# One attention-decode kernel, one core: the large loads move from SyncE's queue to GpSimd's, with an engine's rows joined in one packet

## The chip, the cores and the metric

The kernel runs on one core of one Trainium2 chip. Its time is the device time of one execution in microseconds (us); three executions of the kernel before gave 1303.61 to 1304.71, with a median of 1303.97. A profile is one further execution, recorded by the hardware profiler. A core has a matrix engine (TensorE, in the profile PE, its weight loads PEld), VectorE (DVE), ScalarE (ACT), GpSimd (POOL), SyncE (SP), and 16 DMA engines which bring data from device memory (HBM) to the core's own memory (SBUF, 128 partitions). A load is handed over by one of SP, ACT and POOL, each of which has a queue of its own that it works through in order; the 16 DMA engines then move the data. A load of 128 partitions gives each DMA engine eight rows.

## The reference, cut to what matters

Two tokens (B = 2) of width 512 go through a cached attention block and a two-layer MLP, in f32.

```
y  = layernorm(x);  q = (y @ wq) -> 2 x 32 heads x 128
scores = q . k_cache * 128**-0.5        # k_cache: 2 x 32 x 8192 x 128
o  = softmax(scores) . v_cache          # v_cache: the same shape
h  = x + o @ wo                         # wo: 4096 x 512
h2 = h + gelu(layernorm(layernorm(h)) @ w1 + b1) @ w2 + b2   # 512 -> 1792 -> 512
```

K and V are 268 MB each, and each element is used once. All else together is some 25 MB.

## The kernel before, in words

The work is cut into 32 units: a unit i is a pair of heads g of one token b, so units come in twos (b = 0, then b = 1). The K of a unit is a tile of 128 partitions, 64 KB in each (8 MB), and so is its V. There are three such slots of SBUF (`kv`), taken in turn: wq, K0, K1, V0, K2, V1, K3, V2 and so on, then wo, the last V and the MLP's weights. V of a unit goes into the slot that its K leaves; K of unit i+1 goes into the slot that V of unit i-2 leaves. A load into a slot can be handed over only when the last reader of what lay there is done.

On a K tile, cut into four chunks (32 of a partition's 128 scores each), DVE multiplies a chunk by q (`multiply`, line 464), for the first three chunks POOL adds the upper 64 products of each score to the lower 64 (`halve`, line 468), and DVE sums what is left (`add_up`, line 471). DVE's order within a unit is multiply 0, multiply 1, sum 0, multiply 2, sum 1, multiply 3, sum 2, sum 3. The row maximum, a maximum over partitions (through PE), and four exponentials on ACT follow for two units together; then `values` (PE, lines 241 and 193) multiplies the weights with V. For b = 0 this is done at the end of unit b = 1, and for b = 1 in the middle of the unit after. The middle pairs' PE work is one loop.

The helper `Waits` sees each instruction and puts a semaphore wait on it for whatever it needs. Loads count on 12 semaphores in turn for the hardware queues and 12 for GpSimd's; a load also waits for the load that used its semaphore before.

Which queue hands over what: SP has wq (line 307), all K and V (line 438), wo (line 444), `wlast` (line 456), the biases (line 667), W1 (line 671), W2 (line 675) and the output (line 782). ACT has x. POOL has two gathers with an index list for the rest of wo (line 448), besides its halvings and, at the end, three small fills (lines 688, 691, 710): `zeros`, which the last head's output is written into, `lane`, a small selector, and `wb`, which PE reads in matmuls whose results are not used (`keep_warm`, lines 715 to 717, the first of them inside the last `values`, line 521). The program sets 1024 bytes of a partition aside for the descriptors that GpSimd writes (line 819). It reads the MLP's weights in the order of use: W1 in two loads, W2 in four of 7, 4, 2 and 1 rows of 2 KB in a partition.

The main loop's hand-overs are at its top (lines 601 to 610): V of unit i-1 and K of unit i+1, before any of unit i's work.

Of the kernel before, what the change touches and what calls it, by code (L numbers as in the profile page):

```python
# [22 lines left out]
GH = 3  # L23
SR = 4
LW = 4
LEFT = (((0, 3), (5, 19), (20, 30), (44, 47), (55, 56), (64, 66), (68, 94), (103, 105), (108, 109), (119, 121)),
        ((0, 2), (5, 11), (12, 30), (44, 47), (56, 57), (64, 66), (68, 95), (103, 104), (108, 109), (112, 113),
         (119, 121)))
# [2 lines left out]
def kept(left):  # L31
    at, runs, n = 0, [], 0
    for a, b in (*left, (P, P)):
        if a > at:
            runs.append((at, n, a - at))
            n += a - at
        at = b
    return runs, n
# [234 lines left out]
def tile_decode_block(nc, waits, x, k, v, wq, wo, wog, wol, w1, bias, w2, out):  # L273
    B, H, SK, DH = k.shape
    D = wq.shape[0]
    F = w1.shape[1]
    DC = D // P
# [4 lines left out]
    ROW = NS2 * DH  # L282
# [3 lines left out]
    NU = len(units)  # L286
# [10 lines left out]
    def slot():  # L297
        return kv.tile([P, ROW], F32, name="kv", tag="kv")
# [3 lines left out]
    junk = const.tile([P, 3], F32, name="junk")  # L302
# [1 line left out]
    x2 = const.tile([B, D], F32, name="x2")  # L304
    nc.scalar.dma_start(x2, x)
    wqt = slot()
    nc.sync.dma_start(wqt, wq.rearrange("(p r) n -> p (r n)", r=DC))
    wqs = wqt.rearrange("p (r n) -> p r n", r=DC)

    wlast = wts.tile([P, LW, D], F32, name="wlast")  # L310
    ident = const.tile([P, P], F32, name="ident")
# [7 lines left out]
    oall = const.tile([P, 2, 2 * GP, B], F32, name="oall")  # L319
    NQ = len(LEFT)  # L320
    og = const.tile([P, NQ * SR + LW - TH, B], F32, name="og")
    slots = [kept(x) for x in LEFT]
    first_slot = [sum(n for _, n in slots[:q]) for q in range(len(LEFT))]
    HG = H - LW
    NS = (HG - 4 * GP) * DH // SR
# [4 lines left out]
    pms = {}  # L330
    for x in LEFT:
        if x not in pms:
            pms[x] = const.tile([P, P], F32, name=f"pm{len(pms)}")
            nc.gpsimd.memset(pms[x], 0.0)
            for p0, s0, n in kept(x)[0]:
                nc.gpsimd.tensor_copy(pms[x][:, p0:p0 + n], ident[:, s0:s0 + n])
    pm = [pms[x] for x in LEFT]
    FAR = 4096.0
    ioff = const.tile([P, len(LEFT)], F32, name="ioff")
    for q in range(len(LEFT)):  # L340
# [79 lines left out]
    def make_q(g):  # L420
        QP[g] = psq.tile([P, B, DH], F32, name="qps")
        for b in range(B):
            rows, cols = of_pair(g)
            q = qs[:, (g - 1) % GH, :] if g else q2[rows, cols]
            pe.matmul(QP[g][:, b], pick[:2 * B, b, :], q, start=True, stop=True)
# [4 lines left out]
    for _ in range(SPARE):  # L430
        pe.matmul(rowacc[:, :B], wz, wz, start=True, stop=True)

    def load(src, i, parts):
        g, b = units[i]
        t = slot()
        rows = src[b, 2 * g:2 * g + 2].rearrange("h (p j) d -> (h p) (j d)", j=NS2)
        for s0, n in parts:
            nc.sync.dma_start(t[:, s0 * DH:(s0 + n) * DH], rows[:, s0 * DH:(s0 + n) * DH])
        return t

    def load_wo():
        t = slot()
        n = 2 * GP * D
        nc.sync.dma_start(t[:, :2 * n], wo)
        tv = t[:, :2 * n].rearrange("p (j c) -> p j c", j=2)
        gv = t[:, 2 * n:].rearrange("p (q r n) -> p q r n", q=len(LEFT), n=D)
        for q in range(len(LEFT)):
            nc.gpsimd.indirect_dma_start(
                out=gv[:, q].rearrange("p r n -> p (r n)"), out_offset=None,
                in_=wog,  # L450
                in_offset=bass.IndirectOffsetOnAxis(ap=gidx[:, q:q + 1], axis=0),
                bounds_check=NS - 1, oob_is_err=False)
        return tv.rearrange("p j (r n) -> p j r n", n=D), gv

    def load_last():
        nc.sync.dma_start(wlast.rearrange("p r n -> p (r n)"), wol)

    def chunk(t, c):
        return t[:, c * CH * DH:(c + 1) * CH * DH].rearrange("p (j d) -> p j d", d=DH)

    def multiply(i, c, t):
        g, b = units[i]
        kc = chunk(t, c)
        nc.vector.tensor_tensor(kc, kc, QP[g][:, b, None, :].to_broadcast([P, CH, DH]), op=ALU.mult)  # L464

    def halve(c, t):
        kc = chunk(t, c)
        nc.gpsimd.tensor_tensor(kc[:, :, 0:HP], kc[:, :, 0:HP], kc[:, :, HP:DH], op=ALU.add)  # L468
# [36 lines left out]
    def inverse(g):  # L505
        r = work.tile(list(RL[g].shape), F32, name="rl" if g < GL else "rlp")
        nc.vector.reciprocal(r, RL[g])  # L507
        RL[g] = r

    def by_head(g):  # L510
        r = RL[g]
        RL[g] = work.tile([4, 2], F32, name="rl2")
        nc.vector.tensor_scalar(RL[g], hmask, r, None, op0=ALU.mult)
# [23 lines left out]
    def head_out(g):  # L537
        op, rl = OP.pop(g), RL.pop(g)
        if g < GL:
            nc.vector.tensor_tensor(orow[:, g % GH], op[:, None, :].to_broadcast([4, 2, DH]),  # L540
                                    rl[:, :, None].to_broadcast([4, 2, DH]), op=ALU.mult)
            return
        nc.vector.tensor_tensor(otz[:, :, 0:32:16], *(x.rearrange("p (b s) -> p s b", b=B) for x in (op, rl)),
                                op=ALU.mult)

    def turn(j):
        rows = orow.rearrange("m k e d -> m (k e d)")
        if j < 4:
# [5 lines left out]
            return  # L554
        TP[j] = psm.tile([P, NQ * SR + LW - TH, 2 * B], F32, name="sm")
        at, n = (HG - 4 * GP) * DH, LW - TH
        last = rows[:, at:at + n * DH].rearrange("m (p r) -> m r p", r=n)
# [25 lines left out]
    def placed():  # L583
        nc.vector.tensor_copy(og[:, :NQ * SR], TP.pop(4))

    def project_all(wot, wgt):
        so = so2[0]
        parts = [(oall[:, j, r, :], wot[:, j, r, :]) for j in range(2) for r in range(2 * GP)]
        parts += [(og[:, q * SR + r, :], wgt[:, q, r, :]) for q in range(NQ) for r in range(SR)]
        parts += [(og[:, NQ * SR + h, :], wlast[:, h, :]) for h in range(LW - TH)]  # L590
        n = len(parts)
# [6 lines left out]

    full = [(0, NS2)]
    assert NS2 == NCH * CH  # L600
    KT, VT = {0: load(k, 0, [(0, NS2 // 2), (NS2 // 2, NS2 // 2)])}, {}
    for i, (g, b) in enumerate(units):
        if i == NU - 1:
            wot, wgt = load_wo()
        if i >= 1:
            VT[i - 1] = load(v, i - 1, full)
        if i + 1 < NU:
            KT[i + 1] = load(k, i + 1, full)
        if i == NU - 2:
            load_last()  # L610
        kt = KT.pop(i)
        S[i] = work.tile([P, NS2], F32, name="s", bufs=3)
        for c in range(NCH):
            multiply(i, c, kt)
            if c < NCH - 1:
                halve(c, kt)
            if c == 0:
                if b == 0 and g >= 1:
                    inverse(g - 1)
                if b == 1 and g >= 1:  # L620
                    head_out(g - 1)
                elif b == 1:
                    nc.vector.memset(orow, 0.0)
                if i == NU - 1:
                    turn(4)
            elif c == 1:
                if b == 0 and g >= 1:
                    by_head(g - 1)
                if b == 0 and g % GH == 1:
                    turned(max(g // GH - 1, 0))  # L630
                if i == NU - 1:
                    turned(4)
                if b == 1 and g < GL:
                    make_q(g + 1)
                    if g % GH == GH - 1:
                        stage((g + 1) // GH)
            if c >= 1:
                add_up(i, c - 1, kt, HP)
            if c == 2 and b == 0 and i >= 1:
                values(i - 1, VT.pop(i - 1))  # L640
                gather(g - 1)
                head_sum(g - 1)
                if g == GL:
                    pe.end()
            if c == 2 and i == NU - 1:
                placed()
                project_all(wot, wgt)
        add_up(i, NCH - 1, kt, DH)
        if b == 0 and g % GH == 0 and g < GL:
            pe.round()  # L650
        row_max(i)
        if i == NU - 1:
            row_sum()
        if b == 1:
            all_max(g)
            exps(g)
            values(i - 1, VT.pop(i - 1))
            total(g)
            if g % GH == 0 and g < GL:
                turn(max(g // GH - 1, 0))  # L660
# [7 lines left out]
    w1t = wt[:, 0:DC * F].rearrange("p (c f) -> p c f", c=DC)  # L668
    w1v = w1.rearrange("(p c) f -> p c f", c=DC)
    for c in range(0, DC, 2):  # L670
        nc.sync.dma_start(w1t[:, c:c + 2], w1v[:, c:c + 2])
    w2t = wt[:, DC * F:2 * DC * F].rearrange("p (t d) -> p t d", t=FT)
    w2v = w2.rearrange("(p t) d -> p t d", t=FT)
    for t, n in ((0, 7), (7, 4), (11, 2), (13, 1)):
        nc.sync.dma_start(w2t[:, t:t + n, :], w2v[:, t:t + n, :])

    inverse(GL)
    nc.scalar.activation(junk[:, 0:1], lt4[:, 0:1], AF.Sqrt)
# [154 lines left out]
```

## Time and profile before

| | |
|---|---|
| median of three runs | 1303.97 us (1303.61 to 1304.71) |
| profiled execution, from the first to the last instruction | 1302.4 us |
| moved from HBM | 561.20 MB, mean 431 GB/s |
| busy: DVE, POOL, PE | 951.3, 442.5, 386.7 us |
| chain that ended last: DMA, DVE, PE | 46%, 38%, 13% |

The runs' times include what lies around the span, so the profiled execution's 1302.4 us stands 1.6 us under the median. The busy times of the engines are to be read against the span: none comes near it. The DMA row, the mean busy share of the 16 engines, is the one that does. The profile counts one record for each row that a DMA engine moves and one for each completion.

### The profile page before, as it was taken

How to read it: one execution, taken by the hardware profiler on the slowest of the kernel's cores; microseconds unless marked ns; L12 is line 12 of the kernel's file. 1: busy time of each engine (PE TensorE's matmuls, PEld its weight loads, DVE VectorE, ACT ScalarE, POOL GpSimd, SP SyncE). 2: the span in 40 equal slices, each digit the busy share in tenths (PEclk: the TensorE clock that was granted, in tenths of full speed). 3: DMA queues.
4: the chain of work that ended last, by engine and by line, in shares of the span. 5: the costliest groups of instructions: out<-in, count | busy, mean ns of one | idle time of the engine just before them, and what ended most of it. 6: DMA issues, size and time to landing. Idle time of an engine off the chain costs nothing.

```text
span 1302.4 us, 6774 instructions
## 1 busy us (share of the span) xinstructions
PE 386.7 (30%) x2900; PEld 122.8 (9%) x2900; DVE 951.3 (73%) x411; ACT 51.7 (4%) x172; POOL 442.5 (34%) x138
## 2 busy tenths in 40 slices
PE   3105033330413314033230413323032331403358
PEld 1101000000100001010000101000010100100113
DVE  1988677779777778777778877777976777877752
ACT  0010000000000000000000000000000000000011
POOL 1444422244432234432234442224442224443320
PEclk9556566575666657566665666667566665756669
DMA  9999999999999999999999999999999999999998
GB/s 403 435 449 418 445 423 443 425 435 433 429 439 431 439 431 435 427 443 423 443 427 439 431 431 439 431 437 429 439 427 441 425 439 431 431 439 429 432 426 370
DMA packets 11420, 561.20 MB, mean 431 GB/s; under 512 B 1404, under 2 KB 1412, under 8 KB 1806
## 3 DMA queue, kind: packets, MB, share of 16 engines
q1 hardware_dynamic: 11114, 559.97, 99.5%
q0 software_dynamic: 288, 1.05, 0.2%
q8 instruction: 8, 0.13, 0.0%
q14 instruction: 6, 0.05, 0.0%
q10 hardware_dynamic: 4, 0.00, 0.0%
HBM read 562.06 MB, written 0.00 MB: 432 GB/s over the span
## 4 chain that ended last, share of the span: by engine, by line
DMA 46%; DVE 38%; PE 13%; ACT 1%; issue 1%; POOL 0%; SPq 0%; another core or an unknown queue 0%
DMA kv<-in_k_dram 41%; DVE kv L464 22%; DVE s L471 14%; PE so L241 11%; DMA kv<-in_w_dram 3%; DMA kv<-in_wq_dram 2%; PE sm L241 1%; ACT pt L495 1%; PE so L193 1%; DVE gm L483 0%; DVE mx L478 0%; DVE orow L540 0%; POOL kv L468 0%; DVE qs L418 0%; ACT nb L490 0%
## 5 line engine op out<-in xcount | busy, mean ns | idle before, releaser
L464 DVE TENSOR_TENSOR kv<-kv,qps 128x4096 f32<-128x4096 f32 x128 | 564.0, 4408 | 274.7 <-DMA kv<-in_k_dram 274.6
L468 POOL TENSOR_TENSOR kv<-kv 128x2048 f32<-128x2048 f32 x96 | 433.4, 4522 | 794.8 <-DVE kv L464 452.7
L471 DVE TENSOR_REDUCE s<-kv 128x32 f32<-128x2048 f32 (+1 forms) x128 | 357.2, 2810 | 0.7 <-POOL kv L468 0.3
L241 PE MATMUL so<-kv,pt 128*16 128x512 f32 x1920 | 277.7, 742 | 267.1 <-DMA kv<-in_v_dram 244.9
L241 PE MATMUL sm<-ident,mx 128*1 128x128 f32 x30 | 9.7, 325 | 568.1 <-DVE mx L478 568.1
L241 PEld LDWEIGHTS so<-kv,pt 128*16 128x16 f32 x1920 | 66.1, 113 | 453.9 <-DMA kv<-in_v_dram 246.3
L241 PEld LDWEIGHTS sm<-ident,mx 128*1 128x1 f32 x30 | 2.4, 79 | 574.2 <-DVE mx L478 571.1
L527 ACT ACTIVATE ss<-so 128x512 f32<-128x512 f32 x16 | 9.6, 597 | 553.7 <-PE so L241 516.1
L490 ACT ACTIVATE nb<-sm 128x4 f32<-128x4 f32 x16 | 2.8, 174 | 649.0 <-PE sm L241 646.9
L495 ACT ACTIVATE pt<-s,nb 64x128 f32<-64x128 f32 x64 | 25.5, 399 | 1.7
L193 PE MATMUL qps<-kv,pt 128*16 128x512 f32 x128 | 17.8, 690 | 8.6 <-DMA kv<-in_v_dram 8.6
L241 PE MATMUL sm<-ss,sel 128*4 128x128 f32 x120 | 15.6, 272 | 12.5 <-ACT ss L527 10.7
L404 DVE COPY q<-so 128x512 f32<-128x512 f32 x1 | 0.7, 690 | 19.5 <-PE so L193 19.5
L507 DVE RECIPROCAL rlp<-sm 128x4 f32<-128x4 f32 x1 | 0.2, 181 | 17.5 <-PE sm L193 17.5
L241 PEld LDWEIGHTS sm<-ss,sel 128*4 128x4 f32 x120 | 9.3, 87 | 28.2 <-ACT ss L527 17.3
L483 DVE TENSOR_REDUCE gm<-sm 1x4 f32<-1x256 f32 x16 | 6.6, 412 | 7.3 <-PE sm L241 7.0
L193 PE MATMUL so<-kv,yT 128*4 128x512 f32 x64 | 8.6, 700 | 11.2 <-DMA kv<-in_wq_dram 11.2
L495 ACT ACTIVATION_READ_ACCUMULATOR pt<-s,nb 64x1 f32 x64 | 11.8, 184 | 0.0
L241 PE MATMUL qps<-qs,pick 4*128 4x128 f32 x60 | 11.1, 306 | 0.0
L241 PE MATMUL sm<-gm,srow 1*128 1x4 f32 x30 | 8.7, 359 | 7.6 <-DVE gm L483 7.6
L478 DVE TENSOR_REDUCE mx<-s 128x1 f32<-128x128 f32 x32 | 9.1, 286 | 1.1
L193 PE MATMUL so<-kv,oall 128*2 128x512 f32 x48 | 7.6, 796 | 7.8 <-DMA kv<-in_wo_dram 7.8
(116 smaller groups left out, 130.7 us busy)
## 6 DMA issues: line engine op xcount, KB each, us to landing
kv<-in_k_dram SPq DMA_DIRECT2D x2, 4096.0 KB, 36.5
kv<-in_wo_dram SPq DMA_DIRECT2D x1, 6144.0 KB, 32.2
kv<-in_w_dram SPq DMA_DIRECT2D x3, 1792.0 KB, 34.5
kv<-in_v_dram SPq DMA_DIRECT2D x1, 4096.0 KB, 29.0
kv<-in_v_dram SPq DMA_DIRECT2D x1, 2048.0 KB, 27.3
kv<-in_v_dram SPq DMA_DIRECT2D x1, 1536.0 KB, 26.6
wlast<-in_wol_dram SPq DMA_DIRECT2D x1, 1024.0 KB, 37.1
kv<-in_w_dram SPq DMA_DIRECT2D x1, 1024.0 KB, 40.4
```

The source lines that it names most:

```text
L193: getattr(self.nc.tensor, what)(*aps, **how)
L241: ins = getattr(pe, what)(*aps, **how)
L404: nc.vector.tensor_copy(q2, so2[0])
L464: nc.vector.tensor_tensor(kc, kc, QP[g][:, b, None, :].to_broadcast([P, CH, DH]), op=ALU.mult)
L468: nc.gpsimd.tensor_tensor(kc[:, :, 0:HP], kc[:, :, 0:HP], kc[:, :, HP:DH], op=ALU.add)
L471: nc.vector.tensor_reduce(S[i][:, c * CH:(c + 1) * CH], chunk(t, c)[:, :, 0:n], axis=AX.X, op=ALU.add)
L478: nc.vector.tensor_reduce(MX[g][:, b:b + 1], S[i], axis=AX.X, op=ALU.max)
L483: nc.vector.tensor_reduce(gm, MT.pop(g).rearrange("o b (s p) -> o b s p", s=2), axis=AX.X, op=ALU.max, negate=True)
L490: nc.scalar.activation(nb, GM.pop(g), AF.Copy)
L495: nc.scalar.activation(ptz[b][q, :, 4 * m:4 * m + 4], s[q], AF.Exp, bias=nb[q, b, e:e + 1], scale=SCALE, accum_out=lt4[q, m:m + 1])
L507: nc.vector.reciprocal(r, RL[g])
L527: nc.scalar.activation(SS[g], so2[g == GL], AF.Copy)
```

## The change

Four things change in the program.

- The hand-overs of K, V, wo, `wlast`, W1 and W2 move from SP's queue to GpSimd's, with `single_packet=True`, by which the rows that one DMA engine gets of a load are joined in one packet. wq, the biases and the output stay on SP.
- wq is read in two loads, 56 KB and 8 KB of each partition's 64 KB. GpSimd copies one column of the first part into a scratch tile, so it waits for that part before it hands over K0.
- Before the loop, K0 (in two halves), K1 and V0 are handed over.
- From unit 2 on, V of unit i-1 is still handed over at the top of the unit, but K of unit i+1 only behind GpSimd's first halving of unit i. `wlast` moves with it.

```diff
+QTAIL = 2048
...
     wqt = slot()
-    nc.sync.dma_start(wqt, wq.rearrange("(p r) n -> p (r n)", r=DC))
+    wqv = wq.rearrange("(p r) n -> p (r n)", r=DC)
+    for a, e in ((0, ROW - QTAIL), (ROW - QTAIL, ROW)):
+        nc.sync.dma_start(wqt[:, a:e], wqv[:, a:e])
...
+    def soft(to, of):
+        nc.gpsimd.dma_start(to, of, single_packet=True)
...
         for s0, n in parts:
-            nc.sync.dma_start(t[:, s0 * DH:(s0 + n) * DH], rows[:, s0 * DH:(s0 + n) * DH])
+            cols = slice(s0 * DH, (s0 + n) * DH)
+            soft(t[:, cols], rows[:, cols])
...
-        nc.sync.dma_start(t[:, :2 * n], wo)
+        soft(t[:, :2 * n], wo)
...
-        nc.sync.dma_start(wlast.rearrange("p r n -> p (r n)"), wol)
+        soft(wlast.rearrange("p r n -> p (r n)"), wol)
...
+    nc.gpsimd.tensor_copy(junk[:, 0:1], wqt[:, 0:1])
     KT, VT = {0: load(k, 0, [(0, NS2 // 2), (NS2 // 2, NS2 // 2)])}, {}
+    KT[1] = load(k, 1, full)
+    VT[0] = load(v, 0, full)
     for i, (g, b) in enumerate(units):
         if i == NU - 1:
             wot, wgt = load_wo()
-        if i >= 1:
+        if i >= 2:
             VT[i - 1] = load(v, i - 1, full)
-        if i + 1 < NU:
+        if i == 1:
             KT[i + 1] = load(k, i + 1, full)
-        if i == NU - 2:
-            load_last()
...
             if c < NCH - 1:
                 halve(c, kt)
+            if c == 0 and 2 <= i < NU - 1:
+                KT[i + 1] = load(k, i + 1, full)
+            if c == 0 and i == NU - 2:
+                load_last()
...
-        nc.sync.dma_start(w1t[:, c:c + 2], w1v[:, c:c + 2])
+        soft(w1t[:, c:c + 2], w1v[:, c:c + 2])
...
-        nc.sync.dma_start(w2t[:, t:t + n, :], w2v[:, t:t + n, :])
+        soft(w2t[:, t:t + n, :], w2v[:, t:t + n, :])
```

## The prediction

> **What bounds the kernel now.** I read the page first: the span, the DMA queues, the chain by engine, and the costliest group of instructions (busy us and mean ns, then the idle time before it and for whom).
>
> ```profile
> span 1302.4 us, 6774 instructions
> ...
> DMA packets 11420, 561.20 MB, mean 431 GB/s; under 512 B 1404, under 2 KB 1412, under 8 KB 1806
> ## 3 DMA queue, kind: packets, MB, share of 16 engines
> q1 hardware_dynamic: 11114, 559.97, 99.5%
> ...
> DMA 46%; DVE 38%; PE 13%; ACT 1%; issue 1%; POOL 0%; SPq 0%; another core or an unknown queue 0%
> ...
> L464 DVE TENSOR_TENSOR kv<-kv,qps 128x4096 f32<-128x4096 f32 x128 | 564.0, 4408 | 274.7 <-DMA kv<-in_k_dram 274.6
> ```
>
> SP's queue (q1) alone fills 99.5% of the 16 DMA engines' span. The chain gives DVE 38%, but the row of line 464 shows DVE waiting 274.6 us for K, so the chain runs through DVE only because it steps back to what released a load. Then the chain in order of time (start, us, what).
>
> ```profile
> 0.74 21.91 DMA kv<-in_wq_dram
> ...
> 140.50 4.42 DVE kv L464
> ...
> 1225.37 4.42 DVE kv L464
> ```
>
> The last two are the first work on K3 and K31. Between them lie 56 loads of 8.39 MB: 1084.87 / 56 = 19.37 us each, 433 GB/s. At that rate the page's 561.20 MB take 1296 us of the 1302.4; what is left, 6 us, is the start and the end. So only three things can move the time: the rate of the stream, a hole in it, and the two ends. The profiled span stands 1.6 us under the median of 1303.97; I sum against the span and add 1.6.
>
> **The stream: an engine's rows in one packet.** The page counts a record for each row. What a record costs beside its bytes can be read at the end, where PE waits for W2 piece by piece (timeline: start, us, engine, line, what, idle before and for whom).
>
> ```profile
> 1295.33 1.74 PE L193 MATMUL qps<-kv 128*32 128x128 f32 x56 [0.97 <-DMA kv<-in_w_dram]
> 1297.84 1.08 PE L193 MATMUL qps<-kv 128*32 128x128 f32 x32 [0.77 <-DMA kv<-in_w_dram]
> 1299.12 1.05 PE L193 MATMUL qps<-kv 128*32 128x128 f32 x24 [0.21 <-DMA kv<-in_w_dram]
> ```
>
> The second piece has eight rows of 8 KB for an engine, 64 KB, and took 1297.84 - 1295.33 = 2.51 us; one row of 64 KB takes 19.37 / 8 = 2.42. The third, eight rows of 4 KB, took 1.28 against 1.21. So eight records more cost 0.09 and 0.07 us: 9 to 11 ns a record. Moved are 33 loads of K, 35 of V, one of wo, one of wlast, two of W1 and four of W2: 76, each with eight rows and a completion for an engine. Joining leaves one packet of nine records, 8 x 76 = 608 joints fewer. Bounds: nothing (the cost is the row's own) to 608 x 11 ns = 6.7 us. Each joined row still has a descriptor to be worked through, so not all can go; I take 7 ns, 4.3 us gained.
>
> [...]
>
> **The hand-overs inside the loop.** They move from SP, which does nothing else, into POOL's order of work. One unit, by engine (SP, DVE, POOL, PE):
>
> ```profile
> 92.01 0.33 SPq L438 DMA_DIRECT2D kv<-in_v_dram  x1
> 105.92 0.33 SPq L438 DMA_DIRECT2D kv<-in_k_dram  x1
> ...
> 101.66 4.42 DVE L464 TENSOR_TENSOR kv<-kv,qps 128x4096 f32<-128x4096 f32 x1 [8.48 <-DMA kv<-in_k_dram]
> ...
> 117.26 2.27 DVE L471 TENSOR_REDUCE s<-kv 128x32 f32<-128x2048 f32 x1
> ...
> 106.16 9.00 POOL L468 TENSOR_TENSOR kv<-kv 128x2048 f32<-128x2048 f32 x2 [22.62 <-DVE rl L507]
> ...
> 121.17 8.90 PE L241 MATMUL so<-kv,pt 128*16 128x512 f32 x64 [14.52 <-DMA kv<-in_v_dram]
> ```
>
> And POOL's own order at the end, where it hands over its two gathers today:
>
> ```profile
> 1215.69 1.24 POOL L448 DMA_INDIRECT kv<-in_wog_dram,gidx  x1 [8.76 <-DVE s L471]
> 1217.23 0.99 POOL L448 DMA_INDIRECT kv<-in_wog_dram,gidx  x1 [0.30 <-issue]
> 1229.88 9.16 POOL L468 TENSOR_TENSOR kv<-kv 128x2048 f32<-128x2048 f32 x2 [11.66 <-DVE kv L464]
> 1241.28 4.53 POOL L468 TENSOR_TENSOR kv<-kv 128x2048 f32<-128x2048 f32 x1 [2.24 <-DVE kv L464]
> 1252.74 0.58 POOL L666 MEMSET kv<- 128x576 f32 x1 [6.93 <-PE so L193]
> 1264.66 0.18 POOL L688 MEMSET kv<- 128x96 f32 x1 [11.34 <-PE qps L193]
> 1264.90 0.18 POOL L691 COPY kv<-ident 2x2 f32<-2x2 f32 x1
> 1266.37 0.52 POOL L710 MEMSET kv<- 128x512 bf16 x1 [1.29 <-PE qps L193]
> ```
>
> K2 lands at 101.66, V1 at 121.17. V1 was handed over at 92.01, when K1's sums were done; these come behind that unit's halvings, so POOL is free and V keeps its time and its lead of 9.6 us. K3 was handed over at 105.92, when V0 was free; now it comes behind the first halving, 106.16 + 4.5 = 110.7, plus a hand-over by POOL. The nearest rows for that are the gathers' 0.99 and 1.24 us. So K3 is in the queue at about 111.9, 9 us before V1 is through: no hole, price nothing. Behind it on POOL waits the second halving: 111.9 to 116.4 instead of 110.7 to 115.2, and DVE asks for it at 117.26. Were that cover gone, DVE would be late by the excess, against the 8.48 us that it waits for K anyway. With one user fewer SP is idle; that is worth nothing.
>
> **The start.** Copying a column of wq makes POOL wait for 56 of wq's 64 KB; the 8 KB rows behind (2.51 us by the W2 piece above) must cover the copy, the hand-over and the first byte.
>
> ```profile
> 1.00:2.00 1.00, 0.00 (x0) 0.00 (x0) 0.84 (x5) 1.00 (x1) 0.98 (x3) 1.00 1.40 459
> ```
>
> A copy is 0.2 us, a hand-over 1.0 to 1.24; the first data came 0.3 to 1.3 us behind SP's first hand-over at 0.74 (the row is the stretch from 1 to 2 us; its last two columns are DMA share and GB/s). That is 1.5 to 2.7 us against 2.51, and a wake-up on either side that no row prices: a hole of 0 to 0.5 us, taken as 0.3. Too early costs too: what is left of wq on SP's queue would take turns with packets of half a K. But K0 and K1 behind it feed the engines for 2 x 19.37 us, so q could be 20 us late without a hole. POOL then waits for V0's slot, which is wq's, until PE has made q; its first halving needs q, so the wait is covered. The first 48 KB of wq let PE begin earlier, worth nothing in a stream that is full.
>
> **The end.** POOL now hands over four pieces of V31, two of W1 and four of W2, and only then makes its last fills.
>
> ```profile
> 1256.92 14.22 SPq L675 DMA_DIRECT2D kv<-in_w_dram  x4
> ...
> 1279.17 0.60 PE L193 MATMUL qps<-kv 128*128 128x512 bf16 x2
> 1281.02 2.43 PE L193 MATMUL qps<-kv,pt 128*16 128x512 f32 x16 [1.25 <-DMA kv<-in_v_dram]
> ```
>
> SP's four hand-overs of W2 stretched over 14.22 us, so its queue was full; nobody stood behind it. POOL's ten take about 11 us from 1246 on (its last halving), to 1257 or some us later where a slot is not yet free, and the fills, now at 1264.66 to 1266.9, stay in time. If held as SP's were, to 1271, PE's first use of a fill, 1279.17, is still safe. If held until V31's third piece lands (1281.02), the fills end at 1281 + 1.1 + 0.9 = 1283, and the last values run from 1283.6 to some 1285.5, 2.1 us late; PE's wait for W2 (0.97) takes up half. So 0 to 1.1 us; I take 0.5. [...]
>
> **Sum.** -4.3 + 0 + 0.3 + 0.5 = -3.5: span 1298.9, time 1300.5 us.
>
> **Rivals.** Joining saves nothing or little, since the cost is the row's: the ends' 0.8 us stay, 1304.8; with half of 7 ns, 1302.6. For it: eight rows of one load follow one another without a hole already, and the engines show 99.5%.
>
> Slower: the seam between two loads of GpSimd's queue. SP's loads abut (19.37 us each, busy throughout). If an engine must pick up each of the 76 loads anew, for x a load, the time grows by 76x; from x = 0.08 us it is over 0.2% slower, at 0.2 it gives 1300.5 + 15.2 = 1315.7. Against it: the load is queued 9 us ahead; the two gathers are all that is on that queue today, too little to tell.
>
> Slower at the end: POOL held in the tail and PE cooling as it waits. The rows from 1295.33 on are 3.9 us of matmuls; at half speed that would be 1304.4. Decided by whether the fills come after 1279.17 + 1.2.
>
> The stream runs dry: POOL gets K late by over 9 us, on account of a halving or a wait ahead of it. 31 times 1 us would be 1331; the lead speaks against it.
>
> **Chances.** The forecast, and a larger gain up to 6.7 us (1298.1 with the ends' 0.8), 0.46. Joining saves little 0.20, the cooling tail 0.06, both within 0.2% (about what a measurement of this kernel can tell from no change; 1301.4 to 1306.6). The seam 0.22, run dry 0.06. So faster 0.46, same 0.26, slower 0.28. The likeliest case's own range is 1297.5 to 1301.4; the one that holds 8 in 10 goes from 1297.0 to a seam of 0.11 us, 1309.
>
> **What would show it.** In the profile after: 433 GB/s in mid-stream becomes 434 to 435 and first work on K3 to K31 shrinks from 1084.87 by about 4 us; DVE still waits for K alone; GpSimd's queue carries over 95%. If W2's four hand-overs stretch on POOL, its fills come late and PE waits for POOL near 1279. I am wrong if that interval does not shrink, or if the DMA row shows holes at seams.

## The result

The changed kernel took 1306.12 us (median of 16 runs, 1305.14 to 1310.51) against 1303.78 for the kernel before (16 runs, 1303.51 to 1304.71): 1.0025 times as long, 95% interval 1.0018 to 1.0032. I had forecast 1300.5 and a gain. It also scatters more: 5.4 us between its fastest and slowest run, where the kernel before has 1.2. Ten of its 16 runs lie at 1305.1 to 1306.2 us and six at 1308.3 to 1310.5; the profiled execution, at 1308.3 us with a span of 1307.0, is one of the six.

The page of the changed kernel first: span, records, the queues, and the chain by engine.

```profile
span 1307.0 us, 6773 instructions
...
DMA packets 11500, 561.20 MB, mean 429 GB/s; under 512 B 1420, under 2 KB 1428, under 8 KB 1758
...
q0 software_dynamic: 11168, 552.61, 97.9%
q1 hardware_dynamic: 314, 8.41, 1.5%
...
DMA 70%; DVE 14%; POOL 11%; PE 2%; issue 2%; ACT 0%; DVEq 0%
```

The loads have moved to GpSimd's queue (q0), which now fills 97.9% of the DMA engines' span. The number of records has not fallen (11,420 before; the second load of wq adds its own). Then the chain in order of time (start, us, what).

```profile
0.75 19.56 DMA kv<-in_wq_dram
...
141.42 4.43 DVE kv L471
...
1225.93 4.42 DVE kv L471
...
1257.95 6.48 issue
1264.43 0.53 POOL kv L437
1264.96 9.10 issue
```

First work on K3 to first work on K31 took 1225.93 - 141.42 = 1084.51 us, 0.36 less than before; my 4 us are not there. K3 comes 0.9 us later than before, a loss at the start. And in place of W2's transfer, the end of the chain runs through POOL, which stands still ahead of a hand-over (line 437 is the new hand-over, `soft`). The timeline of PE and of POOL there, each row with what the engine waited for:

```profile
1264.17 9.10 PE L194 MATMUL qps<-kv,pt 128*16 128x512 f32 x64 [7.37 <-DMA kv<-in_v_dram]
1273.20 0.39 PE L194 MATMUL sm<-lt,ones 128*128 128x4 f32 x2
1273.80 3.63 PE L194 MATMUL qps<-kv,pt 128*16 128x512 f32 x32 [0.21 <-DMA kv<-in_v_dram]
1278.70 1.91 PE L194 MATMUL qps<-kv,pt 128*16 128x512 f32 x16 [1.27 <-DMA kv<-in_v_dram]
1284.39 0.38 PE L194 MATMUL qps<-kv 128*128 128x512 bf16 x1 [3.78 <-POOL kv L722]
1284.70 2.98 PE L194 MATMUL qps<-kv,pt 128*16 128x512 f32 x16
...
1301.58 3.26 PE L194 MATMUL qps<-kv 128*32 128x128 f32 x112 [0.28 <-DVE kv L787]
...
1256.90 1.05 POOL L437 DMA_DIRECT2D kv<-in_w_dram  x2
1264.43 0.53 POOL L437 DMA_DIRECT2D kv<-in_w_dram  x1 [6.48 <-issue]
1274.06 0.53 POOL L437 DMA_DIRECT2D kv<-in_w_dram  x1 [9.10 <-issue]
1278.96 0.53 POOL L437 DMA_DIRECT2D kv<-in_w_dram  x1 [4.37 <-issue]
1282.67 0.54 POOL L437 DMA_DIRECT2D kv<-in_w_dram  x1 [3.18 <-issue]
1283.20 0.20 POOL L700 MEMSET kv<- 128x96 f32 x1
1283.47 0.18 POOL L703 COPY kv<-ident 2x2 f32<-2x2 f32 x1
1283.59 0.51 POOL L722 MEMSET kv<- 128x512 bf16 x1
```

POOL's held hand-overs of W2 go at 1264.43, 1274.06 and 1278.96, each 0.26 us after PE could start on V30 (1264.17) or on a piece of V31 (1273.80, 1278.70). So each waits until one more load is through. With the fourth, at 1282.67, POOL stood still 6.48 + 9.10 + 4.37 + 3.18 = 23.13 us. Behind it come the fills, and PE waits 3.78 us for the last of them. Its matmuls then run slowly, and at 1301.58 PE waits for DVE and no longer for W2: W2 lies there, and the time is PE's. The stretch from 1285 to 1292 of the changed kernel (time and count of PE, PEld, DVE, ACT, POOL; then the granted TensorE clock, DMA share, GB/s):

```profile
1285.00:1292.00 7.00, 7.00 (x51) 3.12 (x47) 0.17 (x1) 0.60 (x1) 0.00 (x0) 0.53 1.01 426
```

and of the kernel before:

```profile
1285.00:1292.00 7.00, 6.76 (x81) 2.64 (x84) 1.31 (x5) 1.75 (x3) 0.00 (x0) 1.00 1.01 426
```

At 0.53 of the clock, 51 matmuls take the time of 81. In windows of half a microsecond the clock of the changed kernel falls to 0.50 at about 1285.4 us and is whole again from about 1295.6 us, so it is low for some 10 us.

### The profile page after: what moved, and what is told of

The parts are those of the page before. It is cut to its first block, busy times and chain, and to the rows that moved or that the text cites. A ratio compares the mean times of both kernels' runs of the same rounds, so it can differ in the third digit from the quotient of the medians.

```text
span 1307.0 us, 6773 instructions
## 1 busy us (share of the span) xinstructions
PE 385.7 (30%) x2897; PEld 121.9 (9%) x2900; DVE 951.4 (73%) x411; ACT 51.7 (4%) x172; POOL 484.2 (37%) x215
## 2 busy tenths in 40 slices
DMA packets 11500, 561.20 MB, mean 429 GB/s; under 512 B 1420, under 2 KB 1428, under 8 KB 1758
## 3 DMA queue, kind: packets, MB, share of 16 engines
q0 software_dynamic: 11168, 552.61, 97.9%
## 4 chain that ended last, share of the span: by engine, by line
DMA 70%; DVE 14%; POOL 11%; PE 2%; issue 2%; ACT 0%; DVEq 0%
DMA kv<-in_k_dram 69%; DVE kv L471 12%; POOL kv L475 10%; DVE s L478 2%; DMA kv<-in_wq_dram 1%; PE so L194 1%; PE qps L194 1%; POOL kv L437 0%; PE sm L194 0%; PE rowacc L194 0%; DVE rl L514 0%; DVE q L407 0%; ACT kv L784 0%; POOL kv L678 0%; POOL kv L722 0%
## 5 line engine op out<-in xcount | busy, mean ns | idle before, releaser
L242 PE MATMUL so<-kv,pt 128*16 128x512 f32 x1920 | 273.9, 734 | 267.8 <-DMA kv<-in_v_dram 245.6
L437 POOL DMA_DIRECT2D kv<-in_v_dram x35 | 19.3, 552 | 272.6 <-DVE mx L485 251.6
L437 POOL DMA_DIRECT2D kv<-in_k_dram x33 | 18.8, 570 | 8.7 <-DVE s L478 8.7
L437 POOL DMA_DIRECT2D kv<-in_w_dram x6 | 3.2, 531 | 23.1 <-issue 23.1
```

Source lines behind the costliest of these rows:

```text
L242: ins = getattr(pe, what)(*aps, **how)
L437: nc.gpsimd.dma_start(to, of, single_packet=True)
```

## The experiments

**More room for descriptors.** The theory: the queue's room ends after seven loads, POOL is held, its fills come late, PE waits and its clock falls. The rivals: the queue or its packets are slower, or something else holds POOL.

```diff
-                     dynamic_dma_scratch_size=1024)
+                     dynamic_dma_scratch_size=2048)
```

> The changed kernel with 2048 instead of 1024 bytes set aside for GpSimd's descriptors, and nothing else. Theory A (the queue's room runs out at the end, GpSimd's fills come behind the held hand-overs of W2 at 1283.2 to 1284.1, and PE first waits for them and then runs slower): the four hand-overs of W2 follow one another within 3 us near 1258 to 1262, the fills stand at 1264 to 1268 as before the change, PE does not wait for GpSimd at the last values, and the time falls by 2 to 5 us to some 1303.8 to 1305.2. Theory B (the loss is in the stream: GpSimd's queue or its packets are slower): the time stays at 1305 to 1310. Theory C (the hand-overs are held by something else than room, such as the semaphores taken in turn): they stretch as now and the time stays.

1304.97 us (11 runs, 1304.36 to 1306.42; ratio to before 1.0010, 1.0001 to 1.0019): 1.15 under the changed kernel's median and steadier. I had expected 2 to 5 us less; only the changed kernel's six runs from 1308.3 up stand that far above it. Its timeline of POOL:

```profile
1257.09 3.15 POOL L437 DMA_DIRECT2D kv<-in_w_dram  x6
1265.61 0.18 POOL L700 MEMSET kv<- 128x96 f32 x1 [5.37 <-PE qps L194]
```

Six hand-overs of W1 and W2 in 3.15 us without a pause, and the fills at their old time. The clock from 1285 to 1292 is whole again:

```profile
1285.00:1292.00 7.00, 6.65 (x81) 3.16 (x82) 1.31 (x5) 1.35 (x2) 0.00 (x0) 1.00 1.01 428
```

So room is what held POOL. When it was first held, from 1257.95 us on, V30, four pieces of V31 and two of W1 were underway: seven loads in 1024 bytes. With 2048 bytes the four of W2 went in behind them, the last by 1260.24 us: eleven underway.

**The fills on another engine.** POOL is still held, but no fill stands behind it.

```diff
-    nc.gpsimd.memset(zeros, 0.0)
+    nc.vector.memset(zeros, 0.0)
...
-    nc.gpsimd.tensor_copy(lane[:, 0:32:16], ident[:B, :B])
+    nc.vector.tensor_copy(lane[:, 0:32:16], ident[:B, :B])
...
-    nc.gpsimd.memset(wb, 0.0)
+    nc.vector.memset(wb, 0.0)
```

(The three stand ahead of `inverse(GL)` here.)

> The changed kernel with its three last fills made by DVE, which is idle from 1255 to 1273, ahead of its reciprocal; GpSimd is still held at W2. Theory A: W2's hand-overs stay stretched to 1282.7, as in the changed kernel, but PE no longer waits at the last values and the time falls to 1303.8 to 1305.2, the same as with more room. Theory B: no change, 1305 to 1310. If W2 itself came too late through the held hand-overs, PE would wait for W2's last pieces past 1301 and the time would stay over 1305.

1305.14 us (11 runs, 1304.68 to 1305.64; ratio 1.0011, 1.0002 to 1.0020), as with more room. W2's hand-overs stayed stretched, the last at 1283.11, and cost nothing by themselves. What costs is the work behind them on POOL.

**Late fills alone, on the kernel before.** All loads stay on SP. POOL copies one column of a piece of V31 ahead of its fills, once of the third piece and once of the last.

```diff
+    held = const.tile([P, 1], F32, name="held")
+    nc.gpsimd.tensor_copy(held, vlast[:, 96 * DH:96 * DH + 1])    # or (NS2 - 8) * DH
     zeros = cut(P, (TH + 1) * 32)
```

> The kernel before with one more instruction: GpSimd copies one column of the third piece of V31 ahead of its last fills, so these come at 1281 to 1282.5 with every load still on SyncE's queue. Theory A: PE waits some 3 us for a fill and runs its next matmuls slower; the time rises by 2 to 5 us to 1306 to 1309 and varies more from run to run than before. Theory B: the late fills are hidden behind W1 and W2, as PE waits 0.2 to 1 us there; under 1 us more, at most 1304.8.

> The kernel before with GpSimd's last fills held until the last piece of V31 has landed (1282.4), 1.4 us later than in the run that held them to the third piece. There PE waited 3.3 us and its clock held in about half of the runs (1303.5 to 1304.7) and fell in the others (1306.2 to 1307.7). Theory A (a wait of about 4 us or more lets the clock fall and PE's 14 us of matmuls behind it run slower): PE waits 4.5 to 5 us, the granted clock from 1285 to 1292 is near 0.5 in nearly all runs, and the time is 1306.5 to 1309. If only the lateness counted, it would be 1.4 us over the fast half of the earlier run, 1305.

With the third piece 1304.13 us (11 runs, 1303.53 to 1307.74; ratio 1.0009, 1.0000 to 1.0018), with the last piece 1306.35 (11 runs, 1305.04 to 1309.36; ratio 1.0020, 1.0011 to 1.0029). PE's wait in the first:

```profile
1282.38 0.63 PE L193 MATMUL qps<-kv 128*128 128x512 bf16 x1 [3.26 <-POOL kv L712]
```

and in the second:

```profile
1283.52 1.03 PE L193 MATMUL qps<-kv 128*128 128x512 bf16 x2 [4.20 <-POOL kv L712]
```

The first median lies where I had put fills that are hidden (at most 1304.8 us), not at the 1306 to 1309 of a PE whose matmuls run slower; the second lies just under its 1306.5 to 1309, with a wait of 4.20 us where I had expected 4.5 to 5. Some runs of each are well above its others: three of 11 over 1306 in the first, where the rest stand at 1303.5 to 1304.7, and six of 11 over 1306.3 in the second, where the rest stand at 1305.0 to 1305.8. I first took the low runs for runs in which the clock held. The traces don't show that. The profiled run of the first is the fastest of its 11 (1303.53), and its clock fell too (the stretches 1279 to 1285 and 1285 to 1292):

```profile
1279.00:1285.00 6.00, 2.74 (x17) 0.62 (x18) 0.00 (x0) 0.00 (x0) 0.93 (x4) 0.72 1.01 417
1285.00:1292.00 7.00, 6.84 (x86) 3.02 (x83) 1.15 (x4) 0.60 (x1) 0.00 (x0) 1.00 1.02 432
```

The profiled run of the second is the slowest of its 11 (1309.36):

```profile
1285.00:1292.00 7.00, 7.00 (x43) 2.91 (x35) 0.17 (x1) 0.60 (x1) 0.00 (x0) 0.50 1.00 426
```

In windows of half a microsecond the first run is at 0.50 from about 1281.5 to 1284.9 us, for 3.4 us; the second from about 1282.1 to 1295.8 us, for 13.7 us. So what differs between these two is how long the clock stays low, and no run here shows why it stays. The low runs of the first stand up to 1.0 us over the kernel before (1303.7) and those of the second 1.3 to 2.0; the others of each stand 1 to 4 us over its low ones. Only one run of each has a trace, so that all the others of the upper group are at half clock for as long is likely and not shown. So late fills alone bring a scatter like the changed kernel's, on the old queue.

**Joining.** The changed kernel with `single_packet` left out, with 1024 and with 2048 bytes; and the kernel before with `single_packet=True` on each of SP's loads from K0 to W2.

```diff
-        nc.gpsimd.dma_start(to, of, single_packet=True)
+        nc.gpsimd.dma_start(to, of)
```

> The changed kernel with the rows of a load not joined in one packet, all else as changed. My forecast of 7 ns for each of 608 joints would make it 4.3 us slower than the changed kernel, first work on K3 to K31 growing from 1084.5 to some 1088. If the joint costs nothing (theory D, a record's cost is the row's own) that interval stays within 0.5 us of 1084.5 and the time within the changed kernel's own spread, 1305 to 1310.

> The changed kernel with 2048 bytes for descriptors and the rows not joined, so that joining is compared with the end undisturbed (1304.97 with joined rows). Theory D (a joint costs nothing): 1304.6 to 1305.4, first work on K3 to K31 within 0.5 us of 1084.5 to 1085. The forecast's 7 ns a joint: 1309. [...]

> The kernel before, all on SyncE's queue, with the joining asked for there. By what GpSimd's queue showed (0.2 to 0.5 us over 56 loads) nothing comes of it: 1303.4 to 1304.0, first work on K3 to K31 within 0.5 us of 1084.9. The forecast's 7 ns a joint would be 1299.5.

With the end undisturbed (2048 bytes), joined is 1304.97 and not joined 1304.79 (11 runs, 1304.61 to 1306.40; ratio 1.0008, 0.9999 to 1.0017). On SP joining gives 1303.73 (11 runs; ratio 1.0000, 0.9991 to 1.0009). Not joined with 1024 bytes gave 1309.62 (5 runs, 1305.84 to 1309.97; ratio 1.0034, 1.0021 to 1.0048), inside the changed kernel's scatter; its profiled run waits 4.61 us for the fill. First work on K3 and K31, with 2048 bytes, joined:

```profile
140.87 4.43 DVE kv L471
...
1226.17 4.42 DVE kv L471
```

and not joined:

```profile
140.86 4.43 DVE kv L471
...
1225.87 4.42 DVE kv L471
```

1085.30 against 1085.01 us; with 1024 bytes it is 1084.51 against 1084.74, and before 1084.87. On SP, joined, it is 1084.92 (140.31 to 1225.23). Asking for joining is worth nothing within 0.3 us. The page counts 11,500 records with it and without it, so nothing here shows whether these rows are joined at all.

**The start.** What is left, 1.2 us over the kernel before, should lie between wq and K0. Once K0 goes back to SP behind wq and GpSimd waits for K0's first half; once wq's last part is made larger.

```diff
-    for a, e in ((0, ROW - QTAIL), (ROW - QTAIL, ROW)):
-        nc.sync.dma_start(wqt[:, a:e], wqv[:, a:e])
+    nc.sync.dma_start(wqt, wqv)
...
-    nc.gpsimd.tensor_copy(junk[:, 0:1], wqt[:, 0:1])
-    KT, VT = {0: load(k, 0, [(0, NS2 // 2), (NS2 // 2, NS2 // 2)])}, {}
+    KT, VT = {0: load(k, 0, [(0, NS2 // 2), (NS2 // 2, NS2 // 2)], nc.sync.dma_start)}, {}
+    nc.gpsimd.tensor_copy(junk[:, 0:1], KT[0][:, 0:1])
```

> The changed kernel with 2048 bytes for descriptors; wq is one load again and K0's two halves follow it on SyncE's queue, while GpSimd waits for the first half of K0 before it hands over K1. This takes the hand-over out of the start. If the remaining 1.3 us over the kernel before lie in the hole between wq and K0, K2's first work comes at 101.6 instead of 102.05 to 102.3 and the time falls by 0.4 to 0.8 us to 1304.2 to 1304.6. If they lie elsewhere (GpSimd's queue in general, or the gathers behind wo), it stays at 1304.8 to 1305.2.

> The changed kernel with 2048 bytes for descriptors and wq in rows of 48 and 16 KB, so 4.9 us of wq cover the hand-over of K0 instead of 2.5. If the hole is only too little cover, the same gain as with K0 on SyncE's queue, 0.4 to 0.8 us. If K0's packets come early and take turns with what is left of wq, q comes some 10 us or more later (first multiply past 40 instead of 33 to 34) without a hole in the stream, as K0 and K1 feed it for 39 us: no loss at the end, 1304.2 to 1305.2.

The second (`QTAIL = 4096`, 2048 bytes) took 1303.97 us (11 runs, 1303.71 to 1304.19; ratio 1.0001, 0.9992 to 1.0010): 1.0 us less, where I had expected 0.4 to 0.8, and the rest is gone. The traces' DMA records show the hole: K0's last row is through at 43.10 us in the kernel before, at 43.82 in the changed kernel and 43.52 with 2048 bytes, and at 42.94 with wq in 48 and 16 KB. K2's first work is at

```profile
101.48 4.42 DVE L471 TENSOR_TENSOR kv<-kv,qps 128x4096 f32<-128x4096 f32 x1 [8.47 <-DMA kv<-in_k_dram]
```

where it stood, with 56 and 8 KB, at

```profile
102.05 4.42 DVE L471 TENSOR_TENSOR kv<-kv,qps 128x4096 f32<-128x4096 f32 x1 [8.46 <-DMA kv<-in_k_dram]
```

The first lost 4 us where I expected a gain: 1308.68 (6 runs, 1307.59 to 1312.22; ratio 1.0034, 1.0022 to 1.0046). K0's second half, on SP, and K1, on GpSimd, took turns, at 435 GB/s in all from 30 to 60 us. DVE's timeline, and POOL's:

```profile
55.66 4.42 DVE L470 TENSOR_TENSOR kv<-kv,qps 128x4096 f32<-128x4096 f32 x1 [10.57 <-DMA kv<-in_k_dram]
...
102.71 0.55 POOL L436 DMA_DIRECT2D kv<-in_v_dram  x1 [8.74 <-DVE s L477]
```

DVE got the second half of K0 at 55.66 (44.40 with 2048 bytes and GpSimd's queue alone), was 10 us behind until K1 was done, and freed K1's slot only in time for a hand-over of V1 at 102.71 (92.69 there). K2 was through by then, so the engines had nothing (no byte moved from 100 to 102 us): the hole is there, two loads behind its cause. Here my "20 us late without a hole" is wrong as well: it counts K1's data, not that each later hand-over waits for DVE.

Whether a joined packet holds an engine was tried on the same kernel, with the rows of K1 and of all else on GpSimd's queue not joined:

> The run with K0 on SyncE's queue and K1 on GpSimd's, K1's rows now not joined. There K0's second half landed at 55.6 instead of 43.5, as the two queues took turns. If a joined packet held an engine until it was through, unjoined rows would bring K0's second half at another time, by 5 us or more. If turns are taken row by row in either case, so that joining changes nothing for the engines, it lands within 1 us of 55.6.

```profile
55.51 4.42 DVE L470 TENSOR_TENSOR kv<-kv,qps 128x4096 f32<-128x4096 f32 x1 [10.59 <-DMA kv<-in_k_dram]
```

55.51 and 55.66 (one run, 1309.19 us). Had a joined K1 of 19.4 us held an engine, the half with rows left over would have come behind it. Here the rows for which joining was asked took turns with the other queue's as the unjoined ones did. Either they are not joined, or a joined packet does not hold an engine for 19.4 us; no run tells the two apart.

**Start mended, room not.**

> The changed kernel with wq in rows of 48 and 16 KB instead of 56 and 8, and nothing else; the room for descriptors stays at 1024 bytes. If the two losses are separate, only the start's 1.0 us goes: K2's first work near 101.5, GpSimd still held to some 1282, PE waiting for its fills, a median of 1304.5 to 1306 that scatters upward by 2 to 5 us. If the start's hole were what brings on the late end, it would be as steady as with both mended, 1304.

1305.83 us (11 runs, 1303.84 to 1309.54; ratio 1.0018, 1.0009 to 1.0028). The fastest run is 1.3 us under the changed kernel's, and the scatter stays, so a start without its hole does not bring the fills back in time. The median fell by only 0.29, as six of the 11 runs are over 1305.5. K2's first work was expected near 101.5 and came at 102.20; K0's last row was through at 42.92, as in the run before, so the hole at the start was gone and the later landmark is not steady enough to show it.

## Why the prediction was wrong

The sum was -4.3 + 0 + 0.3 + 0.5 = -3.5. By the runs it is 0 + 0 + 1.0 + 1.15 = 2.15, against 2.34 measured; 0.24 is between the doubly mended kernel (1303.97) and the one before (1303.73 in those runs). The split between the last two terms depends on the order: with the start mended first, the medians give it 0.29 and the room 1.86, as the scatter moves them.

- *The stream, -4.3.* This step failed. 608 joints at 7 ns became nothing within 0.3 us, on either queue. The 9 to 11 ns were read rightly from W2's pieces, as the price of more rows; that 7 of them would go with joining was my estimate and had no row behind it. Whether they stay because they are the row's own cost or because these rows are not joined is open. I had named a saving of nothing as the first rival and gave it 0.20. Without this term the rest of the sum forecasts a loss of 0.8 us.
- *The hand-overs in the loop, 0.* Right. K3 went into the queue at 111.33 + 0.56 = 111.9, as forecast, and the second halving began at 111.91 (111.9):

```profile
111.33 0.56 POOL L437 DMA_DIRECT2D kv<-in_k_dram  x1
...
111.91 4.53 POOL L475 TENSOR_TENSOR kv<-kv 128x2048 f32<-128x2048 f32 x1
```

  The stream did not run dry and no seam showed: 1084.51 us. A hand-over of POOL is 0.55 us, half of the gathers' I went by.
- *The start, 0.3.* Mis-sized: about 1.0. The bound was 0 to 0.5. From the landing of wq's first part (20.31) to the time at which all 16 engines had begun K0 (23.22) the changed kernel's trace has 2.9 us, where I had summed 1.5 to 2.7 without a wake-up. The mechanism and the place were right.
- *The end, 0.5.* Mis-sized: 1.15 in the median, up to 5.5 in single runs. I worked out the held case and had it to 1.1 us (last hand-over behind V31's third piece, fills until 1283; they ended at 1284.1). Then I weighed it lightly and priced PE's lateness alone. In the profiled run, with its wait of 3.78 us, the clock is also at half for some 10 us, and PE's chain of matmuls up to 1301.58 runs through that. Cooling stood among the rivals at 0.06, but it slowed the 3.9 us from 1295.33 on; in the trace those run at a clock of 1.00, and what is slow is the work before them. The test I wrote for it, fills after 1279.17 + 1.2, was met.

The measured time lay within the stated range, but on the slower side, to which I had given 0.28.

## What to carry to other kernels

The room set aside for GpSimd's queue can run out, and then GpSimd itself stands still (here with seven loads underway in 1024 bytes, for 23.13 us in all; with 2048 bytes it did not): count the loads underway at the busiest place, above all at the end, and look at what stands behind the hand-overs. Where a load must follow another across two queues, cover the whole way from landing to first data (2.9 us in the changed kernel), and don't let a load that is waited for take turns with a later one (here that cost 3.7 us). In this stream, which fills the DMA engines with rows of 64 KB, asking for joining won nothing within 0.3 us. And one window at full clock is not enough to say that a clock held (in `late_fills` 1.00 from 1285 to 1292 us, but 0.50 until 1284.9): look at the stretch around the wait.

## What the runs showed of the hardware that I had not expected

- PE's clock fell in each of the five traced runs in which PE waited for a late fill, after waits of 3.26 to 4.61 us: during the wait, or in the changed kernel 1 us behind it. In the traces of the kernel before, `ring2k` and `fills_dve`, whose fills came in time, it stayed at 1.00 from 1278 to 1298 us. What varied is how long it stayed at 0.50: 3.4 us in the fastest run of `late_fills` (wait 3.26 us, 1303.53 us in all), 10 us in the changed kernel (3.78), and 13.7 us with waits of 3.95, 4.20 and 4.61 us (the runs `q16`, `later_fills` and `unjoined`, at 1309.4 to 1309.6). That the length follows the wait is not shown: these are single runs.
- Rows for which joining was asked were still counted row by row in the profile (11,500 records with it and without it), and the other queue's load took turns with them as with unjoined rows: K0's second half came at 55.66 us beside a K1 for which it was asked, at 55.51 beside one for which it was not.
